# A spectral transform, a gated product and slot experts in one kernel: the transform's start and conversions, the last weights' layout and the output products reworked

## The chip, the cores and the metric

The kernel runs on one core of a Trainium2 chip. The metric is device time in microseconds (us) of one execution. The program is run three times; the kernel before took 1694.34 us in the median (1694.19 to 1695.04).

## The reference

Float32 throughout, but three weights and their reductions come as float64. With `x` of 8 x 3072 x 256:

```python
X = np.fft.fft(np.fft.fft(x, axis=1), axis=2).real          # 24576 tokens of 256
y = ((X @ w_a) * (X @ w_b)) @ w_out                          # 256 -> 1536 -> 256
logits = y @ phi                                             # 32 slots: 8 experts of 4
d = exp(logits - logits.max(0)); d /= d.sum(0) + 1e-9
slot_in = (d.T @ y).reshape(8, 4, 256)
slot_out[e] = np.maximum(slot_in[e] @ w1[e], 0) @ w2[e]      # 256 -> 1024 -> 256
c = exp(logits - logits.max(1)); c /= c.sum(1) + 1e-9
out = c @ slot_out                                           # 24576 x 256
```

## The kernel before, in words

The program is straight-line code; each engine executes its own stream in the order in which the Python code issues it (`manual_schedule`). It has four stages.

*Transform* (`_fft`, loop over 8 batches `b`). VectorE folds a batch of `x` (two 1.5 MB pieces `xt`) by the symmetries of the Fourier transform: `fold`, `fold_far`, `fold_odd`, `fold_even`. TensorE multiplies the folded rows with tables: `back_odd` (`tb_odd`), `back_even` of the batch before (`tb_ev`, and with `tb_h` one more product for a single row `hx`). ScalarE and VectorE evict, and the results go to DRAM scratch (`eo`). Row 384 of each batch needs an own small fold, `rows_384`, whose result takes a round trip through DRAM (`rsc`, read back as `rr`).

The nine 1 MB weight pieces (three each of `w_a`, `w_b`, `w_out`, as 64-bit words) are woven into that loop, one per batch: `fetch` loads, `begin` takes the absolute value on ScalarE, `convert` makes 32-bit values in six VectorE instructions (lines 117 to 127; the last adds the low part to the high part), and `use_in` (TensorE products with `fd`, results `wt`) or `use_out` (transposes, products with `phi`, result `m_sb`) uses them. Before the loop one piece is already converted; the ninth is converted in the last batch.

*Main* (`_main`, 24 blocks of 12 tiles). Per tile: twelve 128x512 products `s`, `d` (lines 500 to 502), VectorE, ScalarE and GpSimd form the gated product `g`, `transp` puts it in token order into `ring`, `logits` multiplies `g` with `m_sb`. Per block there is a running softmax over tokens (`soft_step`) and `z_part` adds the weighted tokens into `acc`. The first tile needs `w128`, loaded as `wr` from scratch `wsc`.

*Tail* (`tail`). The last block's softmax, the remaining `z_part`s, the slot inputs, the experts: `hidden` (w1), `turn`, `back` (w2). `w2t` takes the four `ring` buffers, so each 2 MB load waits until the `z_part` that reads its buffer has run. `rp` makes the slot outputs; `so_h` and `so_l` (high part and rest) are laid out with zeros in the rows of the other token groups.

*Output* (`_out`, 8 batches x 3 blocks). Per block twelve products `o_ps` (128 rows, 512 columns: high x high, low x high, high x low), two evictions, one 1 MB store. `cr` loads the softmax weights that the main stage left in scratch `csc`; `ch` and `cl` are their high part and rest.

Of the kernel before, what the change touches and what calls it, by code (L numbers as in the profile page):

```python
# [29 lines left out]
W_ODD, W_EV, W_H = 8 * 384, 4 * 3 * 384 + 3 * 2, 386  # L30
# [15 lines left out]
def _tables():  # L46
# [22 lines left out]
    h = np.zeros((P, W_H))  # L69
    h[0] = np.where((k_0x // 4) % 2 == 0, 1.0, -1.0)  # L70
    ev = [v.transpose(1, 0, 2).reshape(P, -1) for v in (c2, s2, c0, s0)]
    big = np.ascontiguousarray(np.concatenate([odd] + ev + [h], axis=1), np.float32)
# [10 lines left out]
def _places():  # L83


    out = np.concatenate([1 + 4 * np.arange(768), 2 + 8 * np.arange(384), 4 * np.arange(384)])
    out = out.reshape(3, 4, P)
    back = (NSEQ - out)[:, ::-1, ::-1]
    back = np.where(back == NSEQ, 1536, back)
    return np.concatenate([out, back], axis=1).transpose(0, 2, 1).reshape(-1)  # L90
# [15 lines left out]
def _words(nc, pool, w, n):  # L106
# [7 lines left out]
    def rest():  # L114
# [13 lines left out]
        return t  # L128
# [4 lines left out]
def _weights(tc, pools, w_a, w_b, w_out, phi, fdft, wt, wsc, wof, ident, m_sb, mask):  # L133
# [3 lines left out]
    fd = up.tile([P, 2, 2 * P], F32, name="fd")  # L137
    ph = up.tile([P, 2, NS], F32, name="ph")

    def start():  # L140
        nc.scalar.dma_start(fd, fdft.rearrange("p (t c) -> p t c", t=2))
        nc.scalar.dma_start(ph, phi.rearrange("(t p) s -> p t s", p=P))
# [6 lines left out]
    def single(w):  # L149
        if w.dtype != U64:  # L150
            return lambda: w
        a, b = w.shape[1:]
        rest = _words(nc, up, w.rearrange("p a b -> p (a b)"), a * b)
        return lambda: rest().rearrange("p (a b) -> p a b", a=a)
# [32 lines left out]
    def use_out(q, w):  # L187
        nc.scalar.dma_start(wof[:, 4 * q:4 * q + 4], w)
# [19 lines left out]
    for q in range(3):  # L208
        src = w_out[512 * q:512 * q + 512, :].rearrange("(t p) d -> p t d", p=P)
        units.append((lambda src=src: load(src, 4, D), single, lambda w, q=q: use_out(q, w)))  # L210
        for ab, w in ((0, w_a), (1, w_b)):
            src = w[:, 512 * q:512 * q + 512].rearrange("(t p) f -> p t f", p=P)
            units.append((lambda src=src: load(src, 2, 512), single,
                          lambda w, ab=ab, q=q: use_in(ab, q, w)))
# [3 lines left out]
def _fft(tc, ctx, cw, x, x384, w_a, w_b, w_out, phi, tabs, fdft, wsc, wof, eo, eo0, eo1, exu, rsc,  # L218
         ident, m_sb, ex_e, mask):
# [22 lines left out]
    tb_h = cp.tile([P, W_H], F32, name="tb_h")  # L242
    c0cols = cp.tile([P, 7, nb], F32, name="c0cols")
    hx = cp.tile([P, P], F32, name="hx")
# [44 lines left out]
    def even_rows(b, d, r):  # L289
        nc.scalar.copy(d[0:1, 1, 0, 129:D], r[1][:, 129:D])  # L290
        nc.scalar.copy(hx[0:1], r[1][:, 0:P])
        nc.scalar.copy(c0cols[:, 1:7, b], d[:, :, :, P].rearrange("p s t -> p (s t)"))
# [13 lines left out]
    def load_r(b):  # L306
        r = []
        for q in range(2):
            r.append(zp.tile([1, D], F32, tag=f"r{q}", name="rr"))
            nc.sync.dma_start(r[q], rsc[b:b + 1, q])  # L310
        return r
# [27 lines left out]

    def back_even(b, even):  # L340
        for e in range(2):
# [10 lines left out]
            nc.scalar.copy(sg[:, 384:768], pt[:, :384])  # L352
# [4 lines left out]
    def nyquist():  # L357
# [27 lines left out]
    def convert():  # L385

        if not begun:
            return lambda: None
        conv, f = begun.pop(0)
        w = conv()  # L390
        fetch()
        return f(w)

    fetch()
    x_t = {}
    x_t[0, 0] = load_x(0, 0, nc.scalar, 2)
    w384 = zp.tile([P, 4, 3, D], F32, tag="f", name="w384").rearrange(
        "p a i d -> p (a i) d")[0:nb, 0:8]
    nc.sync.dma_start(w384[:, 0:4], x384)
    x_t[0, 1] = load_x(0, 1)  # L400
    start()
    nc.scalar.dma_start(tb_odd.rearrange("p z j s k -> p (z j s k)"), tabs[:, :W_ODD])
    nc.vector.memset(c0cols, 0.0)
    nc.vector.memset(hx, 0.0)
    begin()
    w = rows_384(w384)
    nc.sync.dma_start(rsc, w)
    nc.scalar.dma_start(tb_ev, tabs[:, W_ODD:W_ODD + W_EV])
    nc.scalar.dma_start(tb_h, tabs[:, W_ODD + W_EV:])
    fetch()  # L410
    x_t[1, 0] = load_x(1, 0)
    r = load_r(0)
    nc.sync.dma_start(c0cols[0:1, 0, :].unsqueeze(2),
                      rsc[:, 1, 128:129].rearrange("b o -> o b").unsqueeze(2))
    todo, even_ = [], None
    rest = convert()
    for b in range(nb):
        begin()
        e = zp.tile([P, 2, 2, 3, D], F32, tag="e", name="e")
        for g in range(2):  # L420
# [11 lines left out]
            if todo:  # L432
                todo.pop(0)()
        odd = new("dz")
        fold_odd(odd, e)
        odd_rows(odd, r)
        if b:
            back_even(b - 1, even_)
        rest()
        todo = back_odd(b, odd)  # L440
# [4 lines left out]
        rest = convert()  # L445
        if b + 1 < nb:
            r = load_r(b + 1)
    for finish in todo:
        finish()
    rest()  # L450
    nyquist()
    back_even(nb - 1, even_)
    return wtp, wt


def _main(tc, ctx, wtp, wt, outs, eo, wsc, exu, ident, m_sb, ex_e, csc, nblk, wof, w1, w2):
# [11 lines left out]
    w128 = wpool.tile([P, 2, NFT], F32, name="w128")  # L468
# [105 lines left out]
    def soft_step(k, step):  # L574
# [48 lines left out]
        elif step == "co":  # L623
# [60 lines left out]
    def load_w1s(e, t):  # L684
# [4 lines left out]
        nc.sync.dma_start(tl, w1[e, t * P:t * P + P, :])  # L689
# [18 lines left out]
    def tail(k, rest):  # L708
# [4 lines left out]
        z_part(k - 1, 2, "d0")  # L713
# [104 lines left out]
        none = gp.tile([P, 4, D], F32, tag="g", name="none")[:, 0:2]  # L818
        nc.gpsimd.memset(none, 0.0)
        for t in so_h + so_l:  # L820
            nc.gpsimd.tensor_copy(t, none)
# [6 lines left out]
        rp = [ps.tile([P, D], F32, tag=t, name="rp") for t in ("t", "l")]  # L828
        for st in range(2):
            nc.tensor.matmul(rp[st], fold.rearrange("p z s -> p (z s)"), so, start=True, stop=True)  # L830
        for st in range(2):
            for copy, dst in ((True, so_h[st]), (False, so_l[st])):
                for z in range(2):
                    c = 3 - z if st else z
                    r = slice(NS * c, NS * c + NS)
                    if not copy:
                        nc.vector.tensor_tensor(dst[r, z], rp[st][r], so_h[st][r, z].bitcast(F32),  # L837
                                                ALU.subtract)
                    elif st:
# [18 lines left out]
    wr = p1.tile([2 * NFT, P], F32, name="wr")  # L858
    for ab in range(2):
        nc.sync.dma_start(wr[ab * NFT:ab * NFT + NFT], wsc[ab].rearrange("(t f) -> t f", t=NFT))  # L860
    x_ps = ps.tile([P, 2, NFT], F32, tag="x", name="w_ps")
    nc.tensor.transpose(x_ps.rearrange("p a t -> p (a t)"), wr, ident[:2 * NFT, :2 * NFT])
    nc.vector.tensor_copy(w128, x_ps)
    for n in range(nper + 2):
# [32 lines left out]
def _out(tc, ctx, c_in, first, so_h, so_l, out, nb):  # L897
# [10 lines left out]
    for b in range(nb):  # L908
        h, l = c_t.pop(b)
        for m in range(3):  # L910
# [3 lines left out]
            for st in range(2):  # L914
                for hh in range(2):
                    for x, (cc, so) in enumerate(((h, so_h), (l, so_h), (h, so_l))):
                        nc.tensor.matmul(pt[st][:, hh], cc[:, m, P * hh:P * hh + P],  # L917
                                         so[st], start=(x == 0), stop=(x == 2))
            o = op.tile([P, 8, D], F32, tag="o", name="o")
            if b == 0 and m == 0:  # L920
                for st in range(2):
                    for hh in range(2):
                        eng = nc.vector.tensor_copy if hh else nc.scalar.copy
                        eng(o[:, 4 * st + hh:4 * st + hh + 3:2], pt[st][:, hh])
                        store_half(o, st, hh)
                continue
            for st in range(2):
                eng = nc.scalar.copy if st else nc.vector.tensor_copy
                eng(o[:, 4 * st:4 * st + 4].rearrange("p (c h) d -> p h c d", c=2), pt[st])  # L929
# [3 lines left out]
def _build(tc, x, x384, w_a, w_b, w_out, phi, w1, w2, tabs, fdft, out):  # L933
# [3 lines left out]
    with ExitStack() as ctx, tc.manual_schedule():  # L937
# [10 lines left out]
        csc = dr.tile([nblk, P, 256], F32, name="csc")  # L948
# [4 lines left out]
        mask = kc.tile([P, 1], F32, name="mask")  # L953
        nc.vector.memset(mask, 1.0)
# [69 lines left out]
```

## Time and profile before

| | us |
|---|---|
| median of three runs | 1694.34 |
| the profiled execution | 1694.86 |
| its span in the trace | 1692.1 |
| transform, to the first main product | 0 to 239.4 |
| main | 239.4 to 1582 |
| tail, to the first output product | 1582 to 1620.0 |
| output | 1620.0 to 1692.1 |

Over the span TensorE is busy 97%, VectorE 82%, GpSimd 68%, ScalarE 38%; the DMA engines are busy in the transform and again in tail and output. Shares of the whole span say little here, since each stage has another limit. A timeline row is start, duration, engine, line, operation, output and input, and in brackets the idle time before it with what ended it; `SPq` and `ACTq` are DMA issues. `x8` merges eight instructions that follow each other. A float32 product is recorded as two instructions.

### The profile page before, as it was taken

Reading aid. Unit: us, or ns where it says so; the run is one execution under the profiler, and the core shown is the slowest. Engines: PE = TensorE matmul, PEld = TensorE weight load, DVE = VectorE, ACT = ScalarE, POOL = GpSimd, SP = SyncE. Lnnn points to the kernel's source line nnn. Section 1 sums busy time; section 2 is a strip of 40 time slices with the busy share of each in tenths; the row PEclk is TensorE's granted clock in tenths of the full one; section 3 lists DMA queues with packets and bytes.
Section 4 is the critical chain, followed back from the end, with each engine's and each line's share of the span. In section 5 each row is a group of like instructions: output and inputs, shape, how many; then the busy total and the mean of one; then the engine's idle time right before and its main releaser. Section 6 shows DMA issues by size and latency. Waiting matters only on the chain. (4 is left out here: it accounts for less than half of the span.)

```text
span 1692.1 us, 27733 instructions
## 1 busy us (share of the span) xinstructions
PE 1635.8 (97%) x10544; PEld 1188.7 (70%) x10544; DVE 1395.1 (82%) x2087; ACT 648.0 (38%) x1007; POOL 1147.9 (68%) x979
## 2 busy tenths in 40 slices
PE   3999989999999999999999999999999999999998
PEld 2555557777777777777777777777777777777577
DVE  7999969888888888888888888888888888888533
ACT  1222223434444443444344434444344444344333
POOL 0000028878887888888788878887888888788411
PEclk9999999999999999999999999999999999999999
DMA  9766430000000000000000000000000000003799
GB/s 379 243 232 222 140 125 20 1 23 23 23 1 23 23 23 1 23 23 22 1 23 23 23 1 23 23 23 1 23 23 23 4 20 23 23 5 128 235 339 372
DMA packets 45084, 123.85 MB, mean 73 GB/s; under 512 B 3900, under 2 KB 23531, under 8 KB 39704
## 3 DMA queue, kind: packets, MB, share of 16 engines
q1 hardware_dynamic: 38688, 108.19, 18.3%
q10 hardware_dynamic: 6264, 13.90, 2.1%
q8 instruction: 83, 1.36, 0.3%
q14 instruction: 49, 0.40, 0.1%
HBM read 79.56 MB, written 42.52 MB: 72 GB/s over the span
## 5 line engine op out<-in xcount | busy, mean ns | idle before, releaser
L525 POOL TENSOR_TENSOR db<-s_sb,db 128x512 f32<-128x512 f32 x287 | 378.9, 1320 | 443.9 <-DVE s_sb L516 242.4
L516 DVE SCALAR_TENSOR_TENSOR s_sb<-ub,w,s 128x512 f32<-128x512 f32 x576 | 404.8, 744 | 79.7 <-PE s L502 77.3
L520 ACT COPY db<-d 128x512 f32<-128x512 f32 x288 | 169.8, 589 | 639.4 <-PE d L502 624.6
L526 POOL TENSOR_TENSOR g<-pl 128x512 f32<-128x512 f32 x288 | 392.9, 1364 | 1.8 <-DVE pl L523 1.2
L527 POOL TENSOR_TENSOR g<-s_sb,db 128x512 f32<-128x512 f32 x287 | 372.8, 1299 | 0.0
L551 ACT COPY ring<-t_ps 128x1024 f32<-128x1024 f32 x286 | 290.7, 1016 | 63.8 <-PE t_ps L548 63.8
L548 PE MATMUL t_ps<-ident,g 128*128 128x128 f32 x2296 | 297.0, 272 | 0.0
L548 PEld LDWEIGHTS t_ps<-ident,g 128*128 128x128 f32 x2296 | 267.6, 140 | 40.0 <-issue 0.4
L500 PE MATMUL s<-eoh,wt 128*128 128x512 f32 x576 | 252.9, 439 | 0.4 <-DVE s_sb L516 0.4
L500 PE MATMUL d<-eoh,wt 128*128 128x512 f32 x576 | 228.0, 396 | 0.3 <-DVE s_sb L522 0.3
L501 PE MATMUL d<-eol,wt 128*128 128x512 f32 x576 | 227.8, 395 | 0.0
L502 PE MATMUL s<-eoh,wt 128*128 128x512 f32 x576 | 227.6, 395 | 0.0
L501 PE MATMUL s<-eol,wt 128*128 128x512 f32 x576 | 226.9, 394 | 0.0
L502 PE MATMUL d<-eoh,wt 128*128 128x512 f32 x576 | 226.8, 394 | 0.0
L522 DVE TENSOR_TENSOR s_sb<-s_sb,d 128x512 f32<-128x512 f32 x288 | 197.7, 686 | 9.9
L523 DVE TENSOR_TENSOR pl<-s_sb,d 128x512 f32<-128x512 f32 x288 | 198.1, 688 | 0.5 <-ACT db L520 0.5
L521 DVE TENSOR_TENSOR pl<-s_sb,d 128x512 f32<-128x512 f32 x288 | 197.9, 687 | 0.0
L500 PEld LDWEIGHTS s<-eoh,wt 128*128 128x128 f32 x576 | 108.5, 188 | 71.8 <-issue 21.4
L559 PE MATMUL l_ps<-g,m_sb 128*32 128x256 f32 x2304 | 140.1, 382 | 0.2 <-POOL g L530 0.2
L568 PE MATMUL z_ps<-ring,d_sb 128*32 128x512 f32 x1152 | 136.7, 592 | 0.2 <-ACT d_sb L601 0.2
L500 PEld LDWEIGHTS d<-eoh,wt 128*128 128x128 f32 x576 | 108.2, 188 | 26.9 <-DVE s_sb L522 0.9
L502 PEld LDWEIGHTS d<-eoh,wt 128*128 128x128 f32 x576 | 108.2, 188 | 26.2
(186 smaller groups left out, 1703.8 us busy)
## 6 DMA issues: line engine op xcount, KB each, us to landing
out_dram<-o SPq DMA_DIRECT2D x23, 1024.0 KB
xt<-in_x_dram SPq DMA_DIRECT2D x15, 1536.0 KB
eoraw<-eo_c SPq DMA_DIRECT2D x16, 512.0 KB
w2t<-in_moe_w_dram SPq DMA_DIRECT2D x4, 2048.0 KB
w1t<-in_moe_w_dram SPq DMA_DIRECT2D x3, 2048.0 KB
eo<-so SPq DMA_DIRECT2D x16, 256.0 KB
eoraw<-eo SPq DMA_DIRECT2D x8, 512.0 KB
ub<-eo_c SPq DMA_DIRECT2D x16, 256.0 KB
```

The costliest lines, as they stand in the source:

```text
L500: nc.tensor.matmul(ps_, wt[ft // 4][:, ft % 4, 0, e, ab], h[:, e], start=True, stop=False)
L501: nc.tensor.matmul(ps_, wt[ft // 4][:, ft % 4, 0, e, ab], l[:, e], start=False, stop=False)
L502: nc.tensor.matmul(ps_, wt[ft // 4][:, ft % 4, 1, e, ab], h[:, e], start=False, stop=True)
L516: nc.vector.scalar_tensor_tensor(out=s_sb[:, ab], in0=ub, scalar=w128[:, ab, ft:ft + 1], in1=s_ps[ab], op0=ALU.mult, op1=ALU.add)
L521: nc.vector.tensor_tensor(pl[:, 0], s_sb[:, 0], d_ps[0], ALU.add)
L522: nc.vector.tensor_tensor(am, s_sb[:, 0], d_ps[0], ALU.subtract)
L523: nc.vector.tensor_tensor(pl[:, 1], s_sb[:, 1], d_ps[1], ALU.add)
L525: eng.tensor_tensor(bm, s_sb[:, 1], db, ALU.subtract)
L526: nc.gpsimd.tensor_tensor(g[:, 0:512], pl[:, 0], pl[:, 1], ALU.mult)
L527: eng.tensor_tensor(g[:, 512:1024], am, bm, ALU.mult)
L548: nc.tensor.transpose(t_ps[:, z], g[:, z * P:z * P + P], ident)
L551: nc.scalar.copy(dst, t_ps)
```

## The change

1. *Transform's start.* `x384` and `x` are loaded first, `fd`, `phi`, `tb_odd` and `tb_ev` move from ScalarE's queue to SyncE's; no weight piece is converted before the loop. The nine conversions each stand one place later, and the last (`w_out`) comes after the loop. `begin` moves behind `back_even`.
2. *Conversion.* For `w_a` and `w_b` the low part `wl32` stays apart (`apart`): the add of line 127 goes, `use_in` makes two more float32r products per half with a rounded copy `fdr` of `fd`.
3. *Row 384.* The extra product with `tb_h` goes; its value enters as a bias (`rt`, `r128`) when ScalarE evicts, with even and odd columns apart (`out_0`).
4. *`w128`* is loaded and made at the end of the transform.
5. *Tail.* `z_part` of the last but one block moves ahead of the last logits. `w1` and `w2` lie in DRAM as partition, then row, so that a partition reads 8 KB in one piece (before 4 KB and 1 KB); the host only reorders them. `csc` is laid out by partition, and two loads replace the eight `cr` loads.
6. *Output.* `so_h`, `so_l` have no zeros: each of four token groups uses its own 32 rows, as 24 products of 32 rows and 256 columns per block instead of 12 of 128 rows and 512 columns. One `rp` product and two casts replace two products and eight copies.

```diff
@@ _words
-def _words(nc, pool, w, n):
+def _words(nc, pool, w, n, apart):
...
+        if apart:
+            r2 = pool.tile([P, n], F32R, tag="r2", name="wl32")
+            nc.vector.scalar_tensor_tensor(out=r2, in0=lo, scalar=2.0 ** -52, in1=r,
+                                           op0=ALU.mult, op1=ALU.mult)
+            return t, r2
...
@@ use_in
-            for t in range(2):
-                nc.tensor.matmul(pt, fd[:, t, e * P:e * P + P], w[:, t],
-                                 start=(t == 0), stop=(t == 1))
+            todo = [(fd, v, t) for v in w[:1] for t in range(2)]
+            if w[1] is not None:
+                todo += [(fdr, w[1], t) for t in range(2)]
+            for z, (fd_, v, t) in enumerate(todo):
+                nc.tensor.matmul(pt, fd_[:, t, e * P:e * P + P], v[:, t],
+                                 start=(z == 0), stop=(z + 1 == len(todo)))
...
@@ back_even
-                passes(pt, 386, [(dat(even, 0, i, 0), t_ev("c0", i)) for i in range(3)] + [(hx, tb_h)])
-                nc.scalar.copy(ex_e[:, b:b + 1], pt[:, 384:385])
+                passes(pt, 386, [(dat(even, 0, i, 0), t_ev("c0", i)) for i in range(3)])
+                nc.scalar.activation(ex_e[:, b:b + 1], pt[:, 384:385], ACTF.Identity,
+                                     bias=rt[:, 0, b:b + 1])
+                out_0(sg[:, 384:768], pt, rt[:, :, b])
...
@@ _fft
-    begin()
     w = rows_384(w384)
-    nc.sync.dma_start(rsc, w)
+    nc.scalar.dma_start(rsc, w)
...
+    begin()
     for finish in todo:
         finish()
+    last = convert()
     rest()
+    wr = st.tile([P, 384], F32, tag="ev", name="wr")[0:2 * NFT, 0:P]
...
     nyquist()
     back_even(nb - 1, even_)
+    rest = last()
...
@@ load_w2
-        nc.sync.dma_start(t, w2[2 * q:2 * q + 2].rearrange("e (t p) d -> p (e t) d", p=P)
-                          .rearrange("p (e t) d -> p e t d", e=2))
+        nc.sync.dma_start(t, w2[2 * q:2 * q + 2].rearrange("e p t d -> p e t d"))
...
@@ tail
-        z_part(k - 1, 2, "d0")
...
-        rp = [ps.tile([P, D], F32, tag=t, name="rp") for t in ("t", "l")]
...
+        rp = ps.tile([P, D], F32, tag="t", name="rp")
+        nc.tensor.matmul(rp, fold.rearrange("p z s -> p (z s)"), so, start=True, stop=True)
+        nc.scalar.copy(so_h, rp)
+        nc.vector.tensor_tensor(so_l, rp, so_h.bitcast(F32), ALU.subtract)
...
@@ _main
+        if n == nper:
+            z_part(nblk - 2, 2)
...
@@ _out
-            for st in range(2):
-                for hh in range(2):
-                    for x, (cc, so) in enumerate(((h, so_h), (l, so_h), (h, so_l))):
-                        nc.tensor.matmul(pt[st][:, hh], cc[:, m, P * hh:P * hh + P],
-                                         so[st], start=(x == 0), stop=(x == 2))
+            for hh in range(2):
+                for x, (cc, so) in enumerate(((h, so_h), (l, so_h), (h, so_l))):
+                    for c in range(4):
+                        r = slice(NS * c, NS * c + NS)
+                        nc.tensor.matmul(pt[c // 2][:, c % 2, hh], cc[r, m, P * hh:P * hh + P], so[r],
+                                         start=(x == 0), stop=(x == 2))
```

VectorE, between the small fold of row 384 (line 303, `w`) and the first fold of `x` (`f`), before:

```order
L303 TENSOR_TENSOR w_123<-w_123 8x127
L117 TENSOR_SCALAR wt_155<-wu 128x1024
L119 SCALAR_TENSOR_TENSOR wt_155<-wu,wt_155 128x1024
L121 SCALAR_TENSOR_TENSOR wt_155<-wr_132,wt_155 128x1024
L123 TENSOR_SCALAR wr_132<-wt_155 128x1024
L125 SCALAR_TENSOR_TENSOR wr_132<-wu,wr_132 128x1024
L127 TENSOR_TENSOR wt_155<-wt_155,wr_132 128x1024
L259 TENSOR_TENSOR f<-xt 128x6x127
```

And now; the next two rows on VectorE are the second half of that fold:

```order
L311 TENSOR_TENSOR w_120<-w_120 8x127
L268 TENSOR_TENSOR f<-xt 128x6x127
L269 TENSOR_TENSOR f<-xt 128x6x127
L270 COPY f<-xt 128x12
L268 TENSOR_TENSOR f<-xt 128x6x127
```

The six conversion instructions have gone from ahead of the first fold.

TensorE, from the last even products of the transform (`tb_ev`) to the first main product (`s`), before:

```order
L253 MATMUL pt<-tb_ev,d 128x386 x3
L253 MATMUL pt<-tb_h,hx 128x386
L253 MATMUL pt<-tb_ev,d 128x384 x6
L862 MATMUL w_ps<-ident,wr 128x24
L500 MATMUL s_1269<-eoh,wt 128x512
```

And now, where `wt_1151` is the last piece of `w_out`:

```order
L262 MATMUL pt<-tb_ev,d 128x386 x3
L262 MATMUL pt<-tb_ev,d 128x384 x6
L202 MATMUL pt<-ident,wt_1151 128x128 x8
L478 MATMUL pt<-ident,wr 128x24
L209 MATMUL pt<-ph,wot 128x32 x8
L527 MATMUL s_1290<-eoh,wt 128x512
```

The product with `hx` is gone; the transposes and the `phi` products of the last weight piece now stand between the transform and the main stage.

TensorE, in the last block, from the transposes of the last but one tile (`t_ps`) to the softmax transposes (`y_ps`), before:

```order
L542 MATMUL t_ps<-ident,g 128x128 x8
L559 MATMUL l_ps<-g,m_sb 32x256 x16
L548 MATMUL t_ps<-ident,g 128x128 x8
L568 MATMUL z_ps<-ring,d_sb 32x512 x8
L599 MATMUL y_ps<-ident,dt 128x128 x2
```

And now:

```order
L569 MATMUL t_ps<-ident,g 128x128 x8
L595 MATMUL z_ps<-ring,d_sb 32x512 x8
L586 MATMUL l_ps<-g,m_sb 32x256 x16
L575 MATMUL t_ps<-ident,g 128x128 x8
L626 MATMUL y_ps<-ident,dt 128x128 x2
```

The eight `z_ps` products have moved from behind the logits (`l_ps`) and the last transposes to ahead of them.

## Rows read from the trace of the kernel before

**Rows 1.** Windows of three stages; busy us per engine, granted clock, DMA share, GB/s

```profile
200.00:220.00 20.00, 18.26 (x56) 10.17 (x54) 19.72 (x27) 5.43 (x14) 0.00 (x0) 1.00 0.22 79
...
1600.00:1620.00 20.00, 17.20 (x202) 8.28 (x194) 2.41 (x12) 6.03 (x18) 4.10 (x5) 1.00 1.10 350
1640.00:1660.00 20.00, 20.00 (x90) 16.56 (x89) 8.67 (x8) 10.19 (x11) 5.53 (x3) 1.00 0.95 386
```

**Rows 2.** Timeline of VectorE at the start: start, duration, then the instruction

```profile
11.04 0.68 DVE L296 TENSOR_TENSOR w<-w 8x512 f32<-8x512 f32 x1 [9.85 <-DMA w<-in_x_dram]
...
14.56 0.67 DVE L117 TENSOR_SCALAR wt<-wu 128x1024 uint32<-128x1024 uint32 x1
...
19.86 1.22 DVE L127 TENSOR_TENSOR wt<-wt,wr 128x1024 f32<-128x1024 f32 x1
21.00 0.94 DVE L259 TENSOR_TENSOR f<-xt 128x762 f32<-128x762 f32 x1
```

**Rows 3.** Timeline of VectorE where the transform ends and main begins

```profile
219.98 1.94 DVE L333 TENSOR_TENSOR so<-ev,pt 128x384 f32<-128x384 f32 x4
...
242.12 1.41 DVE L516 SCALAR_TENSOR_TENSOR s_sb<-ub,w,s 128x512 f32<-128x512 f32 x2 [0.20 <-issue]
```

**Rows 4.** Windows of 2 us at the start and in the tail, columns as in Rows 1

```profile
2.00:4.00 2.00, 0.00 (x0) 0.00 (x0) 0.00 (x0) 0.49 (x1) 0.00 (x0) 1.00 0.83 268
4.00:6.00 2.00, 0.00 (x0) 0.00 (x0) 0.00 (x0) 0.79 (x1) 0.00 (x0) 1.00 1.02 417
...
1582.00:1584.00 2.00, 2.00 (x20) 1.14 (x20) 1.16 (x4) 0.42 (x2) 1.79 (x3) 1.00 1.02 422
1604.00:1606.00 2.00, 2.00 (x22) 0.84 (x20) 0.35 (x2) 0.85 (x3) 0.41 (x1) 1.00 1.10 349
```

**Rows 5.** Timeline of SyncE's DMA issues, at the start and at 237 us

```profile
14.66 0.30 SPq L407 DMA_DIRECT2D rsc<-w  x1
...
20.11 0.54 SPq L310 DMA_DIRECT2D rr<-rsc  x2
...
237.14 0.72 SPq L860 DMA_DIRECT2D wr<-wsc  x2
```

**Rows 6.** Timeline of TensorE in the transform and at its end

```profile
104.36 1.87 PE L200 MATMUL pt<-ph,wot 128*128 128x32 f32 x16
...
232.42 0.81 PE L253 MATMUL pt<-tb_h,hx 128*128 128x386 f32 x2
233.07 4.04 PE L253 MATMUL pt<-tb_ev,d 128*128 128x384 f32 x12
239.31 0.21 PE L862 MATMUL w_ps<-ident,wr 24*128 24x24 f32 x1 [2.20 <-DMA wr<-wsc]
...
242.92 0.50 PE L500 MATMUL s<-eoh,wt 128*128 128x512 f32 x1 [0.41 <-DVE s_sb L516]
```

**Rows 7.** Timeline of TensorE in the last block and the tail

```profile
1567.08 1.93 PE L559 MATMUL l_ps<-g,m_sb 128*32 128x256 f32 x32
...
1579.28 2.15 PE L559 MATMUL l_ps<-g,m_sb 128*32 128x256 f32 x28
...
1582.16 1.09 PE L548 MATMUL t_ps<-ident,g 128*128 128x128 f32 x8
1583.18 1.92 PE L568 MATMUL z_ps<-ring,d_sb 128*32 128x512 f32 x16
...
1614.08 3.65 PE L805 MATMUL op<-w2t,ht 128*32 128x256 f32 x60 [1.65 <-DMA w2t<-in_moe_w_dram]
```

**Rows 8.** Groups by line: evictions of the output; weight loads of the tail

```profile
L929 DVE COPY o<-o_ps 128x1024 f32<-128x1024 f32 x23 | 28.2, 1225 | 33.0 <-PE o_ps L917 32.9
...
L796 PEld LDWEIGHTS tp<-ident,h_sb 128*128 128x128 f32 x16 | 1.7, 140 | 2.1 <-issue 2.1
...
L830 PEld LDWEIGHTS rp<-so,fold 128*128 128x128 f32 x4 | 0.7, 189 | 1.1 <-ACT so L827 1.0
...
L738 PEld LDWEIGHTS sp<-ident,lw 1*128 1x128 f32 x1 | 0.1, 134 | 0.6 <-issue 0.6
```

More of the change, by code (lines that the diff above doesn't have):

```diff
@@ L87, in _places @@
     out = out.reshape(3, 4, P)
-    back = (NSEQ - out)[:, ::-1, ::-1]
+    back = NSEQ - out
     back = np.where(back == NSEQ, 1536, back)
@@ L137, in _weights @@
     fd = up.tile([P, 2, 2 * P], F32, name="fd")
+    fdr = up.tile([P, 2, 2 * P], F32R, name="fdr")
     ph = up.tile([P, 2, NS], F32, name="ph")
     def start():
-        nc.scalar.dma_start(fd, fdft.rearrange("p (t c) -> p t c", t=2))
-        nc.scalar.dma_start(ph, phi.rearrange("(t p) s -> p t s", p=P))
+        nc.sync.dma_start(fd, fdft.rearrange("p (t c) -> p t c", t=2))
+        nc.sync.dma_start(ph, phi.rearrange("(t p) s -> p t s", p=P))
+        return lambda: nc.scalar.copy(fdr, fd)
     def load(src, a, b):
@@ L147, in load, with single @@
         return w
-    def single(w):
+    def single(w, apart=False):
         if w.dtype != U64:
-            return lambda: w
+            return lambda: (w, None)
         a, b = w.shape[1:]
-        rest = _words(nc, up, w.rearrange("p a b -> p (a b)"), a * b)
-        return lambda: rest().rearrange("p (a b) -> p a b", a=a)
+        rest = _words(nc, up, w.rearrange("p a b -> p (a b)"), a * b, apart)
+        return lambda: [v and v.rearrange("p (a b) -> p a b", a=a) for v in rest()]
     def use_in(ab, q, w):
@@ L208, in _weights @@
     for q in range(3):
+        for ab, w in ((0, w_a), (1, w_b)):
+            src = w[:, 512 * q:512 * q + 512].rearrange("(t p) f -> p t f", p=P)
+            units.append((lambda src=src: load(src, 2, 512), lambda w: single(w, True),
+                          lambda w, ab=ab, q=q: use_in(ab, q, w)))
         src = w_out[512 * q:512 * q + 512, :].rearrange("(t p) d -> p t d", p=P)
         units.append((lambda src=src: load(src, 4, D), single, lambda w, q=q: use_out(q, w)))
[L211 to L214, printed above, removed]
     return units, start
 def _fft(tc, ctx, cw, x, x384, w_a, w_b, w_out, phi, tabs, fdft, wsc, wof, eo, eo0, eo1, exu, rsc,
-         ident, m_sb, ex_e, mask):
+         ident, m_sb, ex_e, mask, w128):
     nc = tc.nc
@@ L309, in load_r @@
             r.append(zp.tile([1, D], F32, tag=f"r{q}", name="rr"))
-            nc.sync.dma_start(r[q], rsc[b:b + 1, q])
+            eng.dma_start(r[q], rsc[b:b + 1, q])
         return r
@@ L338, in back_odd, with out_0 @@
         return todo
+    def out_0(dst, pt, add):
+        for z in range(2):
+            nc.scalar.activation(dst[:, z::2], pt[:, z:384:2], ACTF.Identity, bias=add[:, z:z + 1])
     def back_even(b, even):
@@ L391, in convert @@
         fetch()
-        return f(w)
-    fetch()
+        return lambda: f(w)
+    w384 = zp.tile([P, 2, 2, 3, D], F32, tag="e", name="w384").rearrange(
+        "p g a i d -> p (g a i) d")[0:nb, 0:8]
+    nc.sync.dma_start(w384[:, 0:4], x384)
     x_t = {}
[L396 to L399, printed above, removed]
+    x_t[0, 0] = load_x(0, 0, nc.sync, 2)
     x_t[0, 1] = load_x(0, 1)
[L401 to L404, printed above, removed]
-    begin()
-    w = rows_384(w384)
-    nc.sync.dma_start(rsc, w)
-    nc.scalar.dma_start(tb_ev, tabs[:, W_ODD:W_ODD + W_EV])
-    nc.scalar.dma_start(tb_h, tabs[:, W_ODD + W_EV:])
+    rounded = start()
+    nc.sync.dma_start(tb_odd.rearrange("p z j s k -> p (z j s k)"), tabs[:, :W_ODD])
     fetch()
     x_t[1, 0] = load_x(1, 0)
-    r = load_r(0)
-    nc.sync.dma_start(c0cols[0:1, 0, :].unsqueeze(2),
-                      rsc[:, 1, 128:129].rearrange("b o -> o b").unsqueeze(2))
+    nc.sync.dma_start(tb_ev, tabs[:, W_ODD:W_ODD + W_EV])
+    w = rows_384(w384)
+    nc.scalar.dma_start(rsc, w)
+    pt = ps.tile([P, 512], F32, tag="ps", name="pt")
+    nc.tensor.transpose(pt[:, :nb], w[:, 1, 0:P], ident[:nb, :nb])
+    for z, s in ((0, 1.0), (1, -1.0)):
+        nc.scalar.activation(rt[:, z], pt[:, :nb], ACTF.Copy, scale=s)
+        nc.scalar.activation(r128[:, z:z + 1], w[:, 1, P:P + 1], ACTF.Copy, scale=s)
+    r = load_r(0, nc.scalar)
     todo, even_ = [], None
-    rest = convert()
+    rest = lambda: None
     for b in range(nb):
-        begin()
         e = zp.tile([P, 2, 2, 3, D], F32, tag="e", name="e")
@@ L444, in _fft, with _main @@
         even_rows(b, even_, r)
-        rest = convert()
+        rest = convert()()
         if b + 1 < nb:
             r = load_r(b + 1)
+    begin()
     for finish in todo:
         finish()
+    last = convert()
     rest()
+    wr = st.tile([P, 384], F32, tag="ev", name="wr")[0:2 * NFT, 0:P]
+    for ab in range(2):
+        nc.sync.dma_start(wr[ab * NFT:ab * NFT + NFT], wsc[ab].rearrange("(t f) -> t f", t=NFT))
     nyquist()
     back_even(nb - 1, even_)
+    rest = last()
+    pt = ps.tile([P, 512], F32, tag="ps", name="pt")
+    nc.tensor.transpose(pt[:, :2 * NFT], wr, ident[:2 * NFT, :2 * NFT])
+    nc.scalar.copy(w128.rearrange("p a t -> p (a t)"), pt[:, :2 * NFT])
+    rest()
     return wtp, wt
-def _main(tc, ctx, wtp, wt, outs, eo, wsc, exu, ident, m_sb, ex_e, csc, nblk, wof, w1, w2):
+def _main(tc, ctx, wtp, wt, w128, outs, eo, wsc, exu, ident, m_sb, ex_e, csc, nblk, wof, w1, w2):
     nc = tc.nc
@@ L817, in tail @@
         cin, so_h, so_l = outs()
[L818 to L821, printed above, removed]
         back(0)
@@ L953, in _build @@
         mask = kc.tile([P, 1], F32, name="mask")
+        w128 = kc.tile([P, 2, NFT], F32, name="w128")
         nc.vector.memset(mask, 1.0)
@@ L982, in cin @@
                 return h, l
-            for b in range(min(8, nb)):
-                load(b)
             return cin, so_h, so_l
         with ExitStack() as c1:
-            cin, first, so_h, so_l = _main(tc, c1, wtp, wt, outs, eo, wsc, exu, ident, m_sb, ex_e, csc,
+            cin, first, so_h, so_l = _main(tc, c1, wtp, wt, w128, outs, eo, wsc, exu, ident, m_sb, ex_e, csc,
                                     nblk, wof, w1, w2)
```

95 lines of the change are left out of this document (37 added, 58 removed).

## The prediction

> **What bounds the kernel now.** I read the stages by windows first, then the timelines at their edges. In the transform VectorE is the bound: 19.72 of 20 us, with TensorE at 18.26 [rows 1]. Main is TensorE's: its products are the same before and after, so I give it nothing. In the tail the DMA engines are at a share of 1.10 while TensorE is nearly full [rows 1]. In the output TensorE has no gap at all (20.00 of 20), but the stores are at a DMA share of 0.95 with 386 GB/s [rows 1]: two limits lie almost on each other, and whoever relieves TensorE there meets the stores next. At the transform's start VectorE stands still for 9.85 us until the small piece of `x` lands [rows 2]; whatever begins earlier there moves everything behind it, as VectorE has no other gap until the last batch.
>
> **The change, part by part.**
>
> *Start.* Before, row 384's fold runs 11.04 to 14.56 (3.52 us), one conversion 14.56 to 21.00, and the first fold of `x` starts at 21.00 [rows 2]. Now `x384` is the first load. Bytes flow from about 2 us [rows 4], and a small load takes some 2.2 us from issue to use (237.14 [rows 5] to 239.31 [rows 6]), so it lands at about 4.2 and its fold ends at 7.7. The first half of the first `x` piece, 0.79 MB at 417 GB/s [rows 4], lands at about 6.4 and the second piece (3.2 MB after 2 us) at about 12, when VectorE reaches it at 13: no wait there. But the tile `e` now lies where row 384's rows were, so the first `fold_far`, 3.7 us after the fold begins, waits until the write of `rsc` has landed. That took 5.45 us behind a full queue (14.66 to 20.11 [rows 5]) and would take about 2.2 on an idle one; it has 3.6, and now stands first on ScalarE's queue. I take 0.3 us of wait out of 0 to 1.85. So the first fold starts at an effective 8.0 instead of 21.0: 13.0 us earlier (10.5 to 14.3). The conversion that stood there isn't free: it comes back behind the loop, below.
>
> *Conversions in the loop.* Line 127 goes for six of the nine pieces; each holds VectorE for 1.14 us (19.86 to 21.00 [rows 2]): 6 x 1.14 = 6.8. TensorE gets four float32r products more per piece (about 0.22 us each, the pace of the output's: 20 us over 90 recorded [rows 1]) and loses `hx`, 0.65 (232.42 to 233.07 [rows 6]). That is +0.25 a batch, while VectorE's batch shrinks by 1.14; with 18.26 of 20 busy TensorE comes to about 97% and may run late for a batch or two, but what VectorE takes from it is read a batch later. If TensorE did bind, some 3 us would be left. I take 6.8 (3 to 6.9).
>
> *End of the transform.* Before, VectorE ends the last batch at 219.98 and multiplies the first tile at 242.12 [rows 3]; in between TensorE runs its last products. They become 0.5 us shorter (two products of 0.65 less, 0.9 more). Then, before, `wr` holds TensorE for 2.20 us [rows 6]; now it is loaded beforehand. In its place stand the last piece's transposes (about 0.9), the wait for ScalarE, which first issues four stores and a copy to DRAM (some 2 us) and copies twice, and the `phi` products, 1.87 [rows 6]. The first main product so starts about 2.4 us later behind the loop's end. Of this the start of main hides a part: VectorE, busy with clearing accumulators, held TensorE until 242.92 [rows 6] and again after. I charge 0.9 us (between +0.5 and -2.4). The deferred conversion itself lies beside 16 us of TensorE products.
>
> *Tail.* Moving `z_part` takes 1.92 us of TensorE work from behind the logits, where it covered the softmax chain, to ahead of them. Before, the logits take 1579.28 to 1582.16, 2.88 us, since they wait for the last `g`; undisturbed they take 1.93 [rows 7]. So they end 1.92 + 1.93 - 2.88 = 1.0 us later, and the chain from there to `d_sb` has no cover to lose but its own length: the rest comes 1.0 us later (0 to 1.9). Against that, `back` waits 1.65 us for `w2t` [rows 7]. The tail's loads ran at 349 GB/s with 1 KB rows; `w1t` with 4 KB rows at 422 [rows 4]. `w2t` in 8 KB pieces should be like the latter, and its first load starts some 4 us sooner, so this wait goes wholly. Then `rp` and the casts: one chain of three steps instead of ten instructions, 0.8 us less. Together 1.45 less (0.5 to 3).
>
> *Output.* Per block 24 products of 256 columns. If four row groups run beside each other, they need the time of 6 x 256 columns, about 0.7 us; one after the other 24 x 0.11 = 2.7, as before. What the row groups' weight loads cost, the trace bounds only. A load of 1 row by 128 columns takes 134 ns, one of 128 by 128 in the same mode 140 [rows 8]: fewer rows buy nothing.
> The Trainium skill ("TensorE: Matmul & The Clock Gate", "LDWEIGHTS (loading the stationary operand)") says the same, that columns and not rows set the time, and these two rows agree; by its P / 1.2 I estimate 24 x 107 ns = 2.6 us of loads a block, so loads alone could eat the gain. The same page's "Measured speedup vs the span model" gives 3.07x for four row groups, which no row here shows; by it the block would take about 0.9 us.
> Both ends lie at or below the present 2.72 us a block (1.05 MB at 386 GB/s [rows 1]), and the evictions need 1.23 [rows 8]. So the stores become the bound: at a share of 1.00 they give 386 / 0.95 = 406 GB/s or 2.58 us, 24 x 0.14 = 3.3 us gained (0 if 386 is already their limit, 5.6 at the loads' 422 GB/s).
>
> *Sum.* 13.0 + 6.8 - 0.9 + 1.45 + 3.3 = 23.65. The profiled execution took 1694.86, so 1671.2; the runs' median is 0.5 lower: **1670.7 us**.
>
> **Rivals.**
>
> *The start gives half.* `x` and `tb_odd` now share one queue with everything else, and each issue can wait for an earlier landing; `rsc` takes its 5.45 us, the second `x` piece comes late, TensorE binds the loop. For it: the DMA engines are full for the first 40 us in any order, 417 GB/s at 1.02 [rows 4]. Against: `x` comes ahead of all else, where it stood behind 1 MB of weights. Then 8 + 3.5 at the front, 1694.3 - 11.5 + 0.9 - 4.75 = about 1679.
>
> *The back gives nothing.* Stores already at their limit and the softmax chain uncovered: 13.0 + 6.8 - 0.9 with 0.5 from the tail, 1675. For it: the share of 0.95 [rows 1] is near full. Against: the loads' 422 at 1.02 [rows 4].
>
> *The row groups run one after the other, with load and product in series.* This is the case that ends slower. Place: the 576 products of the output. A load takes 189 ns [rows 8] and a product of 256 columns 110: 299 ns x 576 = 172 us instead of 65, so 107 us more, less the 20 gained before: about 1781. The change loses as soon as a product with its load takes over 113 + (20.3 / 576 us =) 35 = 148 ns. Against: products on four column groups pass at 57 to 60 ns each with their loads in this kernel, 32 in 1.93 us [rows 7]; nothing shows row groups.
>
> *The change doesn't do what it says:* the row groups don't run beside each other, but loads hide. Then TensorE stays at 2.6 to 2.7 us a block: 1671 to 1674, inside the forecast's own range.
>
> **How the numbers follow.** Forecast, 1665 to 1676 with its own bounds: 0.66 (the back's rival, 1675, lies in this with 0.12 more). Half a start: 0.14, 1674 to 1684. Row groups in series: 0.06. Something else that eats all: 0.02. The range 1663 to 1681 leaves out the slow case, the worst of the half start and a tenth of the forecast's own tails, about 2 in 10. Faster by over 0.2% (3.4 us, what a measurement can tell from no change): 0.92; within: 0.02; slower: 0.06.
>
> **What would show it.** Right: VectorE's first fold of `x` at 7 to 9 us and hardly idle behind it; its conversions of `w_a` and `w_b` in five instructions; the first main product at about 220 to 223; no wait for `w2t`, with a DMA rate near 400 in the tail; in the output gaps on TensorE and a DMA share of 1.0. Wrong: a wait for `rsc` at the first `fold_far`; TensorE without gaps in the transform and VectorE waiting for it; TensorE still full in the output with a block at over 2.7 us. The main stage's length should stay within 1 us; if it moves, the whole sum is off.

## The result, and the profile after

The changed kernel takes 1677.66 us in the median of four runs (1674.26 to 1680.98), the kernel before 1694.26: a ratio of 0.990 (0.988 to 0.992), 16.6 us less where 23.65 were forecast. Its runs lie 6.7 us apart, those of before 0.9. By stages of the profiled executions (1694.86 and 1677.79 us):

| | before | after | gained | forecast |
|---|---|---|---|---|
| to the first main product | 239.44 | 222.24 | 17.2 | 17.4 |
| from there to the last tile's first product | 1335.13 | 1342.80 | -7.7 | 1.5 |
| from there to the first output product | 45.47 | 43.11 | 2.4 | 1.45 |
| output | 72.09 | 67.86 | 4.2 | 3.3 |
| outside the span | 2.7 | 1.8 | 0.9 | 0 |

The forecast's 1.5 in the second row is what main's start was to hide of the later first product (2.4 less 0.9); to main's products it gave nothing, and that stage is the one that lost. The start went as forecast. VectorE's timeline there (start, duration, instruction, idle time before), which answers to [rows 2]:

```profile
6.24 0.93 DVE L268 TENSOR_TENSOR f<-xt 128x762 f32<-128x762 f32 x1
...
11.24 1.83 DVE L276 TENSOR_TENSOR e<-f 128x774 f32<-128x774 f32 x2 [1.32 <-DMA rsc<-w]
```

The first fold starts at 6.24 instead of 21.00; the wait for `rsc` is 1.32 us. In the output, the window that answers to [rows 1] and two neighbouring groups of TensorE's first block, at full clock:

```profile
1640.00:1660.00 20.00, 14.97 (x194) 12.73 (x192) 9.96 (x9) 9.72 (x11) 4.39 (x3) 0.50 1.01 418
```

```profile
1608.83 0.29 PE L921 MATMUL o_ps<-so_h,ch 32*128 32x256 f32 x4
1608.95 0.29 PE L921 MATMUL o_ps<-so_h,cl 32*128 32x256 f32 x4
```

Each row merges the four products of the four row groups, which start together, and the next four start 0.12 us behind them, loads included. So the row groups run beside each other, and a block's six such steps take 0.72 us where nothing else holds TensorE. The stores are the bound (418 GB/s, share 1.01). TensorE's granted clock was 0.50 there (1.2 instead of 2.4 GHz); with gaps left on TensorE (14.97 of 20 us busy), that cost nothing.

What main lost shows in `split_eo`, which once a block casts the next block's input `eoraw` to its high part `eoh` and subtracts that from it to get the rest, `eol`. The subtraction runs on VectorE and reads both inputs from SBUF. Before, with GpSimd beside it:

```profile
448.34 1.73 DVE L488 TENSOR_TENSOR eol<-eoraw,eoh 128x1024 fp32r<-128x1024 f32 x1 [0.25 <-ACT eoh L485]
...
448.94 2.27 POOL L526 TENSOR_TENSOR g<-pl 128x512 f32<-128x512 f32 x1
```

After, VectorE, GpSimd and TensorE in a like block:

```profile
431.91 4.33 DVE L515 TENSOR_TENSOR eol<-eoraw,eoh 128x1024 fp32r<-128x1024 f32 x1 [0.25 <-ACT eoh L512]
...
431.37 1.32 POOL L552 TENSOR_TENSOR db<-s_sb,db 128x512 f32<-128x512 f32 x1
432.61 1.32 POOL L553 TENSOR_TENSOR g<-pl 128x512 f32<-128x512 f32 x1
433.85 1.32 POOL L554 TENSOR_TENSOR g<-s_sb,db 128x512 f32<-128x512 f32 x1
...
438.98 0.50 PE L527 MATMUL s<-eoh,wt 128*128 128x512 f32 x1 [0.21 <-DVE s_sb L543]
440.95 0.50 PE L527 MATMUL d<-eoh,wt 128*128 128x512 f32 x1 [0.30 <-DVE s_sb L549]
```

Before, `eol` ran behind one GpSimd operation, and the next one was stretched (2.27 instead of 1.3 us). After, it ends 1.1 us behind the third of three: VectorE loses 3.1 of the 4.33 us, since `eol` alone takes 1.22, and TensorE, which had no wait in the steady part of main, waits (0.21 and 0.30 us here). The Trainium skill ("SBUF — State Buffer", "Who interferes with whom") says that a VectorE instruction with two SBUF inputs contends with a GpSimd instruction that reads SBUF, and it calls the lock on the ports that they share exclusive. The rows agree: VectorE and GpSimd wait here for whole instructions of each other. Over main, `eol` (count; minimum, median, maximum in ns) before, after, and in the first experiment:

```profile
L488 DVE TENSOR_TENSOR eol<-eoraw,eoh x24: 1224/1720/2010, 237.9 to 1512.0; 128x1024 fp32r<-128x1024 f32 x24
```

```profile
L515 DVE TENSOR_TENSOR eol<-eoraw,eoh x24: 1224/4319/4339, 216.9 to 1501.7; 128x1024 fp32r<-128x1024 f32 x24
```

```profile
L515 DVE TENSOR_TENSOR eol<-eoraw,eoh x24: 1215/1218/2019, 216.7 to 1471.0; 128x1024 fp32r<-128x1024 f32 x24
```

I call a block hit when its `eol` takes over 4 us. In this execution 14 of 23 are (the expectation below says 15): a hit block lasts about 56.70 us, another 55.62, and before each took 55.98. So there are two unforeseen things in main: hits, and products that got quicker.

### The profile page after: what moved, and what is told of

The parts are those of the page before. It is cut to its first block, busy times and chain, and to the rows that moved or that the text cites. A ratio compares the mean times of both kernels' runs of the same rounds, so it can differ in the third digit from the quotient of the medians.

```text
span 1676.0 us, 28264 instructions
## 1 busy us (share of the span) xinstructions
PE 1608.1 (96%) x10837; PEld 1170.6 (70%) x10837; DVE 1406.6 (84%) x2073; ACT 640.6 (38%) x990; POOL 1128.7 (67%) x974
## 4 chain that ended last, share of the span: by engine, by line
PE 79%; DVE 12%; DMA 4%; ACT 2%; issue 2%; POOL 0%; ACTq 0%; SPq 0%; DVEq 0%
PE t_ps L575 13%; PE s L527 8%; PE d L527 8%; PE d L529 8%; PE d L528 7%; PE s L529 7%; PE s L528 7%; PE l_ps L586 6%; PE z_ps L595 6%; PE pt L262 5%; DVE eol L515 4%; DMA out_dram<-o 2%; PE pt L171 1%; ACT eoh L512 1%; DVE acc L598 1%
## 5 line engine op out<-in xcount | busy, mean ns | idle before, releaser
L552 POOL TENSOR_TENSOR db<-s_sb,db 128x512 f32<-128x512 f32 x287 | 372.5, 1298 | 442.0 <-ACT db L547 306.8
L553 POOL TENSOR_TENSOR g<-pl 128x512 f32<-128x512 f32 x288 | 379.3, 1317 | 10.4 <-DVE pl L550 10.1
L527 PEld LDWEIGHTS s<-eoh,wt 128*128 128x128 f32 x576 | 108.7, 189 | 77.9 <-issue 33.1
L527 PEld LDWEIGHTS d<-eoh,wt 128*128 128x128 f32 x576 | 108.4, 188 | 34.2 <-DVE s_sb L549 11.0
L529 PEld LDWEIGHTS s<-eoh,wt 128*128 128x128 f32 x576 | 108.4, 188 | 25.0
```

Of the source, the lines that this page charges most:

```text
L527: nc.tensor.matmul(ps_, wt[ft // 4][:, ft % 4, 0, e, ab], h[:, e], start=True, stop=False)
L529: nc.tensor.matmul(ps_, wt[ft // 4][:, ft % 4, 1, e, ab], h[:, e], start=False, stop=True)
L552: eng.tensor_tensor(bm, s_sb[:, 1], db, ALU.subtract)
L553: nc.gpsimd.tensor_tensor(g[:, 0:512], pl[:, 0], pl[:, 1], ALU.mult)
```

## The experiments

**The hits.** `split_eo` moved to where GpSimd idles some 3.6 us, in the changed kernel:

```diff
-            if p == 9 and k + 1 < nblk:
-                split_eo(k + 1)
...
             run_side(k - 1, side.get(p, []))
+        if n < nper and p == 5 and k + 1 < nblk:
+            split_eo(k + 1)
```

> The changed kernel, with split_eo (the eoh cast and the eol subtraction of the next block) issued in each block's sixth tile behind the z_part, not in its tenth; nothing else differs. Theory port: in 15 of 23 blocks eol takes 4.3 us instead of 1.23 since VectorE stands behind three GpSimd operations, and a hit block lasts 56.70 us against 55.62. In the sixth tile GpSimd idles some 3.6 us, so eol should take 1.2 to 1.9 us everywhere, TensorE should wait for VectorE nowhere in main, and 15 x 1.08 = 16 us should go: 1661 to 1666. Rival start: main is longer because it starts late and at half clock; then the blocks stay as they are and the time stays at 1674 to 1681.

1662.76 us (1662.27 to 1663.44), ratio 0.982 (0.980 to 0.983). No hit, no wait of TensorE in the steady part of main; main lasts 1326.78 instead of 1342.80, 16.0 less. The 14 hits at 1.08 us are 15.1 of that; the rest lies in the first block, at whose start the clock stood at half for longer in the changed kernel. Of the gain the tail gave 1.7 back (44.80 instead of 43.11 us), since here TensorE's clock fell to half in it:

```profile
1572.00:1576.00 4.00, 3.70 (x21) 1.03 (x24) 1.05 (x3) 0.93 (x4) 0.00 (x0) 0.57 1.01 418
```

The changed kernel had 1.00 in every window of its tail.

The same move in the kernel before:

> The kernel before with the same move of split_eo to the sixth tile. Theory port: before, eol took 1.2 to 2.0 us and TensorE had no wait in main, so there is nothing to gain: 1694 within 1 us, blocks of 55.98 us. Rival: the 55.98 us a block of before already hold a hidden cost of this place (the changed kernel's undisturbed blocks take 55.62); then 23 x 0.36 = 8 us go, 1686.

1694.14, ratio 1.000 (0.999 to 1.001): nothing to gain there, and its blocks stay at 55.98.

What makes the hits appear? The change also makes one copy of ScalarE's two `ct` copies per block, which the list of the change leaves out. In two copies again:

> The changed kernel with ScalarE's ct copy in two halves of 64 partitions as before (0.36 + 0.37 us instead of 0.38); nothing else. Theory: the phase between VectorE and GpSimd is set by ScalarE's work at a block's start, and the copy restores the phase of before; then hits go and the time is 1661 to 1667. Rival: the phase comes from elsewhere (the start of main, the layout in memory), and hits stay: 1674 to 1681, with some 15 eol of 4.3 us.

1679.17 (1673.95 to 1679.56): the rival; ScalarE's copy is not it. The profiled execution is the fastest of these, 1673.95 with 10 hits. Against 1677.79 with 14 that is 3.84 us for 4 hits, near their 1.08 each, so a varying number of hits may be what spreads the changed kernel's runs. One trace per kernel doesn't show it, and runs without hits spread too (1657.15 to 1661.85 in the last experiment below).

**The place of `eoh` and `eol`.** `w128` now lies in front of main's tiles and shifts them by 96 bytes. The kernel before with that shift alone:

```diff
         mask = kc.tile([P, 1], F32, name="mask")
+        pad = kc.tile([P, 24], F32, name="pad")
+        nc.vector.memset(pad, 0.0)
```

> The kernel before with one unused tile of 96 bytes per partition behind mask, so that eoh and eol lie 96 bytes further, at the same places as in the changed kernel (there w128 moved in front of them); no work changes but a 0.06 us memset. Theory place: TensorE's eoh and eol products are quicker there (0.2285 against 0.232 us from one to the next), an undisturbed block lasts 55.62 instead of 55.98 us, and that shift also changes where VectorE meets GpSimd: some 15 eol of 4.3 us, main 5 to 8 us longer, 1699 to 1702. Rival A: the quicker products come from the place, the hits from elsewhere: 1686. Rival B: neither does: 1694 within 1.

1685.03, ratio 0.995 (0.993 to 0.996): an unused tile gains 9.3 us, without hits, and blocks last 55.57 us. Rival A held. The time goes from the products that read `eoh` and `eol` and not from the others. One of the former and the transposes, before and here (number, busy us, mean ns):

```profile
L501 PE MATMUL d<-eol,wt 128*128 128x512 f32 x514 | 203.3, 395 | 0.0
L548 PE MATMUL t_ps<-ident,g 128*128 128x128 f32 x2056 | 265.9, 272 | 0.0
```

```profile
L501 PE MATMUL d<-eol,wt 128*128 128x512 f32 x518 | 202.7, 391 | 0.0
L548 PE MATMUL t_ps<-ident,g 128*128 128x128 f32 x2075 | 268.5, 272 | 0.0
```

With the move of `split_eo` too:

> The kernel before with the 96 byte tile and with split_eo in the sixth tile. Theory place: quicker products without hits, blocks of 55.62 us, 24 x 0.36 = 8.4 us gained: 1685 to 1686.5. Rival B (the place does nothing): 1694 within 1.

1684.53: as forecast. To see whether the place counts within 128 bytes, 32 bytes more in the changed kernel (with the move):

> The changed kernel with split_eo in the sixth tile (1662.8), and in it an unused tile of 32 bytes per partition behind w128, so that everything of main on that side lies 32 bytes further: eoh and eol 128 bytes behind their places of before (35136 and 39232; before 35008 and 39104; changed 35104 and 39200). Theory period: what makes their products quick or slow is the place within 128 bytes; then this is the slow place again, blocks of 55.98 us, 24 x 0.36 = 8.4 us more, 1671. Rival: 128 bytes are not the period or eoh's place isn't the cause; blocks stay at 55.62, 1662 to 1664.

1677.60 (1676.76 to 1680.09), slower than either side expected. VectorE's `eol` rows of two neighbouring blocks give a block's length: before with the move, the changed kernel with the move, and the latter with 32 bytes more:

```profile
433.56 1.22 DVE L488 TENSOR_TENSOR eol<-eoraw,eoh 128x1024 fp32r<-128x1024 f32 x1
...
489.54 1.22 DVE L488 TENSOR_TENSOR eol<-eoraw,eoh 128x1024 fp32r<-128x1024 f32 x1
```

```profile
414.28 1.22 DVE L515 TENSOR_TENSOR eol<-eoraw,eoh 128x1024 fp32r<-128x1024 f32 x1
...
469.89 1.22 DVE L515 TENSOR_TENSOR eol<-eoraw,eoh 128x1024 fp32r<-128x1024 f32 x1
```

```profile
416.17 1.22 DVE L515 TENSOR_TENSOR eol<-eoraw,eoh 128x1024 fp32r<-128x1024 f32 x1
...
472.29 1.22 DVE L515 TENSOR_TENSOR eol<-eoraw,eoh 128x1024 fp32r<-128x1024 f32 x1
```

55.98, 55.61 and 56.12 us for the same work. The 32 bytes cost 12.1 us in main; the other 2 to 3 lie in the tail, at half clock for longer. The place counts. But the blocks are longer than the 55.98 of the place 128 bytes ahead, so a period of 128 bytes is not shown; which tile's place decides isn't either, as other tiles moved along.

**The output** (on the changed kernel with the move, as all that follow but one): twelve products with zeros again, as in the old lines of the diff, with eight casts.

> The changed kernel with split_eo in the sixth tile (1662.8), and in it the output products as before: 12 products of 128 rows and 512 columns a block, with zeros, eight small casts. Theory stores: before, TensorE bound the output at 2.72 us a block and 386 GB/s; with row groups the stores do, at 416 to 418 GB/s and 2.5 us. So 24 x 0.2 = 5 us and 0.8 for the casts come back: 1667 to 1669. Rival: the stores were the limit in both; then only the casts come back, 1663 to 1664.

1672.00, ratio 0.987 (0.986 to 0.989), 9.2 more where 4 to 6 were expected. The steady window is the one of before, TensorE full and 387 GB/s:

```profile
1640.00:1660.00 20.00, 20.00 (x90) 16.57 (x89) 8.57 (x7) 9.37 (x10) 3.70 (x2) 1.00 0.94 387
```

So the stores' theory holds, with 24 x 0.2 us; the surplus lies in the first block (waits of 0.92 and 0.96 for my eight casts, some ten products at half clock).

**The conversions**: `single(w)` without `apart`.

> The changed kernel with split_eo in the sixth tile (1662.8), and in it the low part of w_a and w_b added on VectorE again (six additions of 1.14 us come back, 24 float32r products of 0.22 go from TensorE). Theory VectorE: it is busy 24.7 of 25 us in every batch of the transform, so 6 x 1.14 = 6.8 us come back, less up to 0.9 behind the loop where TensorE's last piece has four products fewer: 1668.5 to 1669.5. Rival TensorE: it has no gap in most batches of the changed kernel and binds; then the additions cost 3 us or less, 1663 to 1666.

1670.85, ratio 0.986 (0.985 to 0.988). The first main product comes 7.4 us later than with the move alone: VectorE bound the transform, TensorE did not. The rest is a longer stretch of half clock in the tail.

**The tail.** The old layout of `w1` and `w2`:

> The changed kernel with split_eo in the sixth tile (1662.8), and in it w1 and w2 laid out in DRAM as before (a partition reads 4 KB and 1 KB pieces instead of 8 KB). Theory layout: the tail's loads go at some 349 GB/s instead of 412 to 424, the last w2t piece lands later and back waits for it as before (1.65 us then; the tail is now 1 to 2 us shorter ahead of it): 1.5 to 3.5 us more, 1664.3 to 1666.3. Rival: the earlier start of the loads alone removed the wait; then 1662 to 1664.

1663.24, ratio 0.982 (0.981 to 0.983): the rival. Windows of the loads in the tail, of the changed kernel and of this one, whose tail begins 15.8 us earlier:

```profile
1576.00:1580.00 4.00, 3.33 (x33) 1.02 (x33) 1.68 (x5) 1.55 (x5) 0.00 (x0) 1.00 1.00 418
```

```profile
1576.00:1580.00 4.00, 4.00 (x36) 1.40 (x32) 0.17 (x1) 1.41 (x4) 0.00 (x0) 0.87 1.10 348
```

The loads do go at 418 instead of 348 GB/s, but `back` waits for `w2t` in neither. `z_part` back in the tail:

> The changed kernel with split_eo in the sixth tile (1662.8), and in it the z_part of the last but one block back in the tail behind the softmax sum. Theory move: ahead of the logits it fills the 0.95 us for which they wait, while in the tail it covers the softmax chain, where TensorE now waits 0.90 and 0.82 us: a gain of 1.0 us by the forecast, so 1663.8. Rival: it covered these waits wholly (1.7 us), and moving it gained nothing: 1661.5 to 1663.

1661.61, ratio 0.981 (0.980 to 0.982): no difference in the time clear of its spread. The trace does show one. From the last tile's first product to the last block's first `z_part` it takes 11.34 us here, 11.37 before and 11.89 in the changed kernel:

```profile
1549.01 0.48 PE L527 MATMUL s<-eoh,wt 128*128 128x512 f32 x1
...
1560.35 3.64 PE L595 MATMUL z_ps<-ring,d_sb 128*32 128x512 f32 x32 [0.16 <-ACT d_sb L628]
```

```profile
1565.04 0.48 PE L527 MATMUL s<-eoh,wt 128*128 128x512 f32 x1
...
1576.93 3.64 PE L595 MATMUL z_ps<-ring,d_sb 128*32 128x512 f32 x32
```

So moving `z_part` ahead costs 0.5 us there. `back` doesn't wait here either. No run undoes layout and move together, so either may remove that wait alone, or a third thing may, such as the two loads in place of the eight `cr` loads.

**The end of the transform.** Five DMA issues from ScalarE to SyncE (in the changed kernel as it is):

> The changed kernel with the last batch's four sg stores and the last wof store issued by SyncE instead of ScalarE; nothing else. Theory: at the end of the transform ScalarE issues DMAs for about 2 us ahead of the wot copies, TensorE waits 1.93 us, its clock falls to half at 220 us, and the phi products take 3.32 instead of 1.87 and the first 10 main products 0.43 instead of 0.23 each. Without the issues the wait is under 0.5 us and the clock stays at 1.00, so the first main product comes 3 to 3.4 us earlier (219 instead of 222.2) and tile 2 some 4 us earlier. Rival: the wait is another's (the wot copies wait for the transposes, or the stores on SyncE hold up the loads of the first block), and the first main product stays within 1 us of 222. The blocks' hits may change either way, so the stage is read, not the sum.

1680.60. The wait for `wot` went, but the load of the first block's `eoraw`, which stood at 206.40 on SyncE's queue, was now issued behind the stores at 219.15, and the first main product came at 226.62:

```profile
219.15 0.41 SPq L504 DMA_DIRECT2D eoraw<-eo  x1
```

```profile
226.62 0.79 PE L528 MATMUL s<-eoh,wt 128*128 128x512 f32 x1 [6.46 <-DVE eoh L515]
```

That is the rival's mechanism, and it cost more than the rival said. The later start of main did not end the hits: 11 blocks have them. Then the same issues kept on ScalarE, but behind the `wot` copies (with the move of `split_eo`):

> The changed kernel with split_eo in the sixth tile (1662.8), and in it ScalarE issues the last sg stores and the last wof store behind the wot copies instead of ahead of them (SyncE's queue is left as it is). Theory: the wot copies come some 1.8 us earlier, TensorE's wait of 1.93 us falls to 0.5 or less, the phi products run at full clock (1.9 instead of 3.3 us), and the first main product comes at 218 to 219 instead of 221 to 222; main's first tile may then wait for VectorE's clears, so 2 to 3.5 us less in all: 1659.3 to 1660.8. Rival: VectorE (eoh, eol, fold and the clears, until 220.9) holds the first tile then, and under 1 us is left: 1662 to 1663.

1660.48 (1657.15 to 1661.85), ratio 0.980 (0.979 to 0.981): the fastest version, 2.3 us under the one with the move alone by the medians, with intervals of the ratios that overlap. TensorE in the changed kernel, then here:

```profile
219.11 3.32 PE L209 MATMUL pt<-ph,wot 128*128 128x32 f32 x16 [1.93 <-ACT wot L203]
222.24 0.77 PE L527 MATMUL s<-eoh,wt 128*128 128x512 f32 x1
```

```profile
217.25 2.23 PE L212 MATMUL pt<-ph,wot 128*128 128x32 f32 x16
219.32 0.48 PE L540 MATMUL s<-eoh,wt 128*128 128x512 f32 x1
...
220.11 0.57 PE L540 MATMUL s<-eoh,wt 128*128 128x512 f32 x1
```

The wait is gone, and the first main product comes at 219.32 instead of 222.24 (221.23 with the move alone). Yet the clock falls all the same, behind the small transposes and the 32-column products; TensorE was busy for 1.85 and 2.00 us of the two windows of 2 us before. It is not the change's alone either: the kernel before kept full clock at the start of main (1.00 from 240 to 242 us), and with only the 96 bytes it had 0.50 there. The windows of 220 to 222 us, the changed kernel and this one, granted clock in the third column from the end:

```profile
220.00:222.00 2.00, 2.00 (x12) 2.00 (x12) 0.87 (x1) 0.00 (x0) 0.00 (x0) 0.51 0.41 160
```

```profile
220.00:222.00 2.00, 2.00 (x7) 1.57 (x6) 1.87 (x3) 0.00 (x0) 0.00 (x0) 0.54 0.81 316
```

## Why the prediction was right or wrong

- *"Main is TensorE's: its products are the same before and after, so I give it nothing."* The step that failed, and with it the prediction's own sign that main's length should stay within 1 us: it grew by 7.7. The shift of 96 bytes gave some 8.5 us (23 blocks of 55.61 instead of 55.98), hits took 15.1, and the first block lost about 0.7. The collision could have been read in the kernel before (1.73 and 2.27 us instead of 1.22 and 1.3); what makes it worse, and the shift in memory, stood in no row that I had.
- *Start*, 13.0: the fold effectively starts at 6.24 + 1.32 = 7.56 instead of 8.0, so 13.4. The wait was 1.32 instead of 0.3, inside its bounds; a wait for `rsc` stood among the signs of being wrong, but it took back only a tenth of the gain.
- *Conversions*, 6.8: shown by the run without them, 7.4. What the 0.6 above six additions is stays open.
- *End of the transform*, -0.9 (+0.5 to -2.4): mis-sized. The prediction let VectorE end the last batch at 219.98; that is the start of four instructions, which end at 221.92. In the changed kernel they end at 200.96:

```profile
198.95 2.01 DVE L341 TENSOR_TENSOR so<-ev,pt 128x384 f32<-128x384 f32 x4
```

  From there to the first main product it takes 21.3 us instead of 17.5, so -3.8 where -2.4 was forecast, and main's start hid nothing (a block later it is another 0.67 late). The clock was not in the sum: `phi` took 3.32 instead of 1.87, and with the same instructions 2.47 in the first experiment.
- *Tail*, 1.45: 2.4. From the start of `back` to `rp` it takes 8.39 instead of 10.62 us, 2.2 less, of which the wait of 1.65 is most. From `rp` to the first output product it takes 1.16 instead of 1.80, so 0.64 for the casts instead of 0.8. Moving `z_part` cost 0.5 instead of 1.0. The layout is not shown to be needed: with the old one `back` didn't wait either. TensorE before, then after:

```profile
1607.62 3.66 PE L805 MATMUL op<-w2t,ht 128*32 128x256 f32 x64
...
1618.24 1.13 PE L830 MATMUL rp<-so,fold 128*128 128x256 f32 x4 [0.52 <-ACT so L827]
1620.04 0.47 PE L917 MATMUL o_ps<-so_h,ch 128*128 128x512 f32 x1 [0.67 <-DVE so_h L842]
```

```profile
1598.60 3.66 PE L827 MATMUL op<-w2t,ht 128*32 128x256 f32 x64
...
1606.99 0.70 PE L847 MATMUL rp<-so,fold 128*128 128x256 f32 x2 [0.55 <-ACT so L845]
1608.15 0.39 PE L921 MATMUL o_ps<-so_h,ch 32*128 32x256 f32 x4 [0.46 <-ACT so_h L848]
```

- *Output*, 3.3: 4.2, as the stores run at 418, not 406 GB/s. The row groups run beside each other and their loads are hidden: the estimate of 2.6 us of loads a block, one after the other, is refuted by 0.72 for loads and products together.
- The sum of what the change does on purpose came close: with the same shift and without hits the two kernels take 1684.53 and 1662.76, 21.8 us apart where 23.65 were forecast. That is in part luck, for the terms' errors cancel (start 0.4, conversions 0.6, end of the transform -2.9, tail 0.9, output 0.9). That the measured time lies in the range is luck too: the range reaches so far up for the half start, which did not happen, and the time came there for a cause that none of the rivals named.

Open: why VectorE gets in behind one GpSimd operation in some blocks and behind three in others. In the shifted kernel of before and in the changed one `eol` starts 0.53 us behind GpSimd's operation, and takes 1.84 us in the one, 4.32 mostly in the other. So neither that offset alone nor the place in memory alone decides it.

## What to carry to other kernels

Where VectorE and GpSimd both run from SBUF nearly all the time, put VectorE's long two-input operations where GpSimd idles: here meeting GpSimd cost 15 us in a part of the kernel that the change was not meant to touch. Before crediting an edit, compare the length of a repeated block that it doesn't touch, and try the shift that its new tiles bring by an unused tile of that size.

## What the runs showed of the hardware

The same products took 55.57 to 56.12 us a block by where their tiles lie, 1%, in steps of 32 to 96 bytes. An `eol` that meets GpSimd at the same offset ran behind one operation in some blocks (1.84 us) and behind three in others (4.32 us). Four row groups of 32 rows run beside each other, loads included: 24 products of 256 columns in 0.72 us at full clock. TensorE's clock fell to half with TensorE busy for 3.85 of the 4 us ahead, behind 2.5 us of 24- and 32-column products.
